# Attention and two MLPs on one core: the first two heads prepared one at a time, their similarities computed in token rows, the order of the first slots rewritten

## The chip, the cores and the metric

The kernel runs on one core of one Trainium2 chip. The metric is the device time of one execution in microseconds (us).

## The reference

The inputs are q, k, v of shape (2, 8, 768, 64), 16 centroids for each of the 8 heads, and the weights of two MLPs; part of the inputs is scaled by 8.

```python
q_assign = argmax(einsum(q / |q|, centroids / |centroids|))    # per token, of 16 clusters; k_assign alike
mask = q_assign[..., :, None] == k_assign[..., None, :]
scores = where(mask, 0.125 * q @ k.T, -1e9)
attn = softmax(scores) @ v                                     # 16 heads of 768 tokens
x = attn as (1536, 512)
x = ((x @ w1) * (x @ w2)) @ w3 @ w_out                         # d_ff 1024
out = softplus(x @ w_in) @ w_o2                                # d_ff 2048
```

## The kernel before

The program has three stages: attention over 16 heads, in 8 pairs; the first MLP; the second. While attention runs, w3 @ w_out is multiplied out once (24 pieces of weights, `wseq`), so that the first MLP has one product less. The MLP stages are not touched by the change.

**One head** has two tiles, `q` and `k` (`QT`, `KT`), of 128 partitions by 2 by 768. In plane 0, rows 0 to 63 hold the high parts of the transposed q or k, rows 64 to 95 a part of the low parts, and rows 96 to 127 the mask rows (one-hot cluster numbers, scaled by 2**100 on one side, so that pairs of tokens of different clusters get a huge score). Plane 1 holds the rest of the low parts, and row 96 of `q` there takes the row minima.

**Preparing a pair.** `load_qk` loads raw q and k (tile `rawqk`); `t1_pe` transposes them on TensorE in four units (head j, half of the tokens), and `t1_ev` splits each into `H` (ScalarE) and `L` (VectorE, L321). `t_dma` copies `H` and `L` into the rows of `q` and `k` by seven DMAs a head (1.15 MB) on SP's queue. `norm_sq`, `norm_sum`, `norm_root` and `norm_rec` make the inverse norms. `sims_pe` multiplies `H` and `L` of both heads with the centroids (`cst`), `sims_ev` copies the result to `sT`, `simsT_pe` turns it into token rows, `assign` finds the first cluster with the largest value (L406 to L420, VectorE) and writes the one-hot tile `oh`, `back_pe` transposes it, `back_ev` scales it into `sg`, and `m_dma` copies `sg` into the mask rows of both heads. Head 0 alone gets plane 0 by engine copies (`t_first`), and its mask rows are written by ScalarE straight from PSUM (L438).

**The slots.** Attention is written out by hand as a loop over 106 slots s. A head has six slots, each for 128 queries: `mx_pe(s)` (L623, their scores against all keys, into `mb`, or `sb` for odd s below 9) and `mx_red(s)` (L632, VectorE: their row minimum). Nine slots later (ML = 9) come `st_pe` (L653, transposed scores of that slot's share, into `sb`) and `st_exp` (L660, ScalarE), and one more slot later `av_pe` (L668, times v). After a head's six minima, `m_row` transposes them and a DMA puts them into row 96 of `q`; `st_pe` of that head needs it. The tables `PE1`, `EV1` say in which slot pair 1 is prepared, `PE`, `EV` (by `steps`) the same for the later pairs. `w_step` advances the 24 weight pieces from slot 9 on, a new piece every 2.5 slots; `w_load` loads them (0.5 MB each). From slot 76 (`WSLOT`) on, the first weights of the MLP are decoded.

Everything inside this loop keeps the written order on each engine; SP's queue issues its DMAs in the written order too. Three PSUM banks (`rb`) are handed around by `take` and `give`, first given, first taken.

Of the kernel before, what the change touches and what calls it, by code (L numbers as in the profile page):

```python
# [27 lines left out]
def fused_kernel(ctx: ExitStack, tc, q, k, v, centroids, w1, w2, w3, wo, w_in, w_o2, out):  # L28
# [175 lines left out]
    def centroid_load():  # L204
        PR["cw"] = ap1.tile([P, D], F32, name="cw")
        dma_in(PR["cw"], centroids.rearrange("h c d -> (h c) d"))

    def centroid_prep():
# [24 lines left out]

    def centroid_turn():
# [4 lines left out]
        for ni, sc in enumerate((-8.0, 1.0)):  # L239
            rows = slice(64 * ni, 64 * ni + 64)  # L240
            mv = m[rows, :P].rearrange("p (g j c) -> p g j c", j=2, c=NCL)
            cv = cst[rows].rearrange("p (g j) x -> p g j x", j=2)
            for j in range(2):
                o = 64 * ni + 32 * j
                hi, lo = cv[:, :, j, o : o + NCL], cv[:, :, j, o + NCL : o + 2 * NCL]
                nc.vector.tensor_scalar(
                    out=hi, in0=mv[:, :, j, :], scalar1=sc, scalar2=None, op0=ALU.mult
                )
                nc.vector.scalar_tensor_tensor(
                    out=lo, in0=mv[:, :, j, :], scalar=sc, in1=f32(hi),  # L250
                    op0=ALU.mult, op1=ALU.subtract,
                )
# [27 lines left out]
    def norm_root(pi):  # L280

        fl = PR["n", pi].rearrange("p t c n j -> p t (c n j)")
        nc.vector.tensor_scalar_max(fl[:, 1], fl[:, 0], 1e-30)
        nc.scalar.activation(fl[:, 2], fl[:, 1], AF.Ln)
        nc.scalar.activation(fl[:, 1], fl[:, 2], AF.Exp, scale=0.5)

    def norm_rec(pi, i):
        fl = PR["n", pi].rearrange("p t c n j -> p t (c n j)")
        if i == 0:
            nc.vector.reciprocal(fl[:, 2], fl[:, 1])  # L290
        elif i == 1:
            nc.gpsimd.tensor_tensor(out=fl[:, 0], in0=fl[:, 0], in1=fl[:, 2], op=ALU.mult)
            nc.gpsimd.tensor_tensor(out=fl[:, 0], in0=fl[:, 0], in1=fl[:, 1], op=ALU.add)
        else:
            nc.vector.tensor_scalar(
                out=fl[:, 2], in0=fl[:, 0], scalar1=0.5, scalar2=1e-6,
                op0=ALU.mult, op1=ALU.add,
            )
            nc.vector.reciprocal(fl[:, 3], fl[:, 2])

    def t1_pe(pi, u):
# [5 lines left out]
        m = take()  # L307
# [7 lines left out]
    def t1_ev(pi, u):  # L315
# [881 lines left out]
```

## Time and profile before

| | us |
|---|---|
| three runs | 842.25, 843.08, 843.41 |
| median | 843.08 |
| profiled execution | 842.76 |
| its span | 840.9 |
| TensorE busy in the span | 796.8 (95%) |
| VectorE, ScalarE, GpSimd busy | 450.6, 396.5, 240.7 |

The span lies inside the execution's time: 1.86 us of the 842.76 are outside it. TensorE (PE) is busy for 95% of the span; the page's line of forty slices (21 us each) shows where it is not: the digits start with 3, 6, 7, 9, stand at 9 after that, and end with 7.

### The profile page before, as it was taken

Reading aid. Unit: us, or ns where it says so; the run is one execution under the profiler, and the core shown is the slowest. Engines: PE = TensorE matmul, PEld = TensorE weight load, DVE = VectorE, ACT = ScalarE, POOL = GpSimd, SP = SyncE. Lnnn points to the kernel's source line nnn. Section 1 sums busy time; section 2 is a strip of 40 time slices with the busy share of each in tenths; the row PEclk is TensorE's granted clock in tenths of the full one; section 3 lists DMA queues with packets and bytes.
Section 4 is the critical chain, followed back from the end, with each engine's and each line's share of the span. In section 5 each row is a group of like instructions: output and inputs, shape, how many; then the busy total and the mean of one; then the engine's idle time right before and its main releaser. Section 6 shows DMA issues by size and latency. Waiting matters only on the chain.

```text
span 840.9 us, 10003 instructions
## 1 busy us (share of the span) xinstructions
PE 796.8 (95%) x3553; PEld 635.5 (76%) x3553; DVE 450.6 (54%) x754; ACT 396.5 (47%) x683; POOL 240.7 (29%) x232
## 2 busy tenths in 40 slices
PE   3679999989999999999999999999998999999997
PEld 2457777867777777778888888887786888888886
DVE  5867565475756565335332343345878644454443
ACT  3345445455453445455333245345555544454443
POOL 4145241245223122145201213222444222222220
PEclk9679999999999999999999999999999999999999
DMA  6875665465552564026301224330210100001001
GB/s 162 203 154 154 161 147 161 122 148 157 152 121 67 133 156 120 21 90 204 127 1 50 83 69 130 120 101 1 75 51 1 50 1 1 1 12 39 1 0 51
DMA packets 77490, 75.60 MB, mean 90 GB/s; under 512 B 46336, under 2 KB 62848, under 8 KB 77440
## 3 DMA queue, kind: packets, MB, share of 16 engines
q1 hardware_dynamic: 75476, 73.84, 32.5%
q10 hardware_dynamic: 1964, 1.12, 0.5%
q8 instruction: 28, 0.46, 0.2%
q14 instruction: 22, 0.18, 0.1%
HBM read 50.41 MB, written 3.24 MB: 64 GB/s over the span
## 4 chain that ended last, share of the span: by engine, by line
PE 77%; DVE 13%; DMA 3%; ACT 3%; SPq 2%; issue 2%; POOL 1%; DVEq 0%; ACTq 0%; POOLq 0%
PE avb L668 11%; PE rb L834 8%; PE sb L834 8%; PE sb L653 6%; PE sb L1059 6%; PE mb L1128 6%; PE rb L1059 5%; PE rb L533 5%; PE mb L856 4%; PE mb L623 3%; PE rb L1128 3%; PE avb L1128 3%; DVE mn L632 2%; PE avb L856 2%; PE rb L856 2%
## 5 line engine op out<-in xcount | busy, mean ns | idle before, releaser
L668 PE MATMUL avb<-E,v 128*128 128x384 f32 x384 | 142.7, 494 | 0.4 <-ACT t L61 0.4
L632 DVE TENSOR_REDUCE mn<-mb 128x1 f32<-128x768 f32 x92 | 87.7, 953 | 103.4 <-PE mb L623 103.0
L76 POOL TENSOR_TENSOR u<-u,t 128x512 f32<-128x512 f32 x47 | 66.2, 1409 | 173.1 <-DVE u L1082 173.1
L660 ACT ACTIVATE E<-sb 128x768 f32<-128x768 f32 x96 | 77.6, 808 | 70.1 <-PE sb L653 69.2
L653 PE MATMUL sb<-q,k 128*128 128x384 f32 (+1 forms) x384 | 91.4, 361 | 4.5 <-ACT E L660 4.5
L668 PEld LDWEIGHTS avb<-E,v 128*128 128x128 f32 x384 | 71.9, 192 | 28.7 <-ACT t L61 2.3
L653 PEld LDWEIGHTS sb<-q,k 128*128 128x128 f32 (+1 forms) x384 | 67.3, 194 | 9.6 <-ACT E L660 7.2
L623 PE MATMUL mb<-k,q 128*128 128x384 f32 x184 | 65.9, 440 | 8.0 <-DVE mn L632 4.1
L1059 PE MATMUL sb<-ys,wh_i 128*128 128x512 f32 x192 | 64.1, 395 | 3.6 <-ACT t L1070 2.9
L1072 DVE TENSOR_SCALAR u<-t 128x512 f32<-128x512 f32 x48 | 25.5, 531 | 71.3 <-ACT t L1071 71.3
L1059 PE MATMUL rb<-ys,wh_i 128*128 128x512 f32 x192 | 63.4, 392 | 0.0
L834 PE MATMUL rb<-xs,wh 128*128 128x512 f32 x192 | 61.7, 393 | 0.0
L834 PE MATMUL sb<-xs,wh 128*128 128x512 f32 x192 | 61.7, 392 | 0.0
L76 POOL TENSOR_TENSOR wl_o<-d_o,wh_o 128x512 fp32r<-128x512 f32 x16 | 21.2, 1327 | 122.3 <-ACT wh_o L61 116.2
L623 PEld LDWEIGHTS mb<-k,q 128*128 128x128 f32 x184 | 34.1, 198 | 26.7 <-DVE mn L632 7.2
L1081 ACT ACTIVATE u<-u 128x512 f32<-128x512 f32 x48 | 30.4, 633 | 42.4 <-DVE t L1078 42.2
L715 POOL TENSOR_TENSOR xT<-t,R 64x384 f32<-64x384 f32 x32 | 33.3, 1061 | 52.6 <-DMA R<-rd 52.3
L79 DVE TENSOR_TENSOR gl<-u,gh 128x512 fp32r<-128x512 f32 x48 | 37.8, 788 | 15.7 <-ACT gh L61 15.2
L1059 PEld LDWEIGHTS sb<-ys,wh_i 128*128 128x128 f32 x192 | 35.9, 188 | 13.3 <-ACT t L1070 3.9
L1059 PEld LDWEIGHTS rb<-ys,wh_i 128*128 128x128 f32 x192 | 36.1, 188 | 8.0
L834 PEld LDWEIGHTS rb<-xs,wh 128*128 128x128 f32 x192 | 36.1, 188 | 7.8
L834 PEld LDWEIGHTS sb<-xs,wh 128*128 128x128 f32 x192 | 36.1, 188 | 7.8
(202 smaller groups left out, 1730.9 us busy)
## 6 DMA issues: line engine op xcount, KB each, us to landing
w3r<-in_moe_w_dram SPq DMA_DIRECT2D x16, 512.0 KB
w12r<-in_moe_w_dram SPq DMA_DIRECT2D x16, 512.0 KB
wir<-in_moe_w_in_dram SPq DMA_DIRECT2D x16, 512.0 KB
wor<-in_moe_w_out_dram SPq DMA_DIRECT2D x16, 512.0 KB
q<-H SPq DMA_DIRECT2D x15, 384.0 KB
w3r<-in_moe_w_out_dram SPq DMA_DIRECT2D x8, 512.0 KB
k<-L SPq DMA_DIRECT2D x16, 192.0 KB
v<-in_v_dram SPq DMA_DIRECT2D x16, 192.0 KB
```

The costliest lines, as they stand in the source:

```text
L76: nc.gpsimd.tensor_tensor(out=o, in0=i, in1=hi, op=ALU.subtract)
L79: return nc.vector.tensor_tensor(out=o, in0=i, in1=hi, op=ALU.subtract)
L533: nc.tensor.matmul(m, a[:, ks], bb, start=(mc == 0 and x == 0), stop=(mc == NK - 1 and x == 2))
L623: nc.tensor.matmul(bank[:, hf, :HALF], QT[g][:, 0, c * P : (c + 1) * P], KT[g][:, 0, hf * HALF : (hf + 1) * HALF], start=True, stop=True,)
L632: nc.vector.tensor_reduce(out=MN[g][:, c : c + 1], in_=mx_bank(s)[:, :, :HALF], op=ALU.min, axis=AX.XY)
L653: nc.tensor.matmul(sbank[:, i, :HALF], KT[g][: P - 31 * n, n, ks], QT[g][: P - 31 * n, n, qs], start=(n == 0), stop=(n == 1),)
L660: nc.scalar.activation(E[j], sbank[:, :, :HALF], AF.Exp, scale=-1.0)
L668: nc.tensor.matmul(avbank[:, :HALF], V[g][:, 2 * kp + i, :], e[:, i, :], start=(kp == 0 and i == 0), stop=(kp == 2 and i == 1),)
L834: nc.tensor.matmul(bk[:, :BLK], a[:, sl], bb, start=(n == 0), stop=(n == 3 * CC - 1))
L856: nc.tensor.matmul(ybank[e][:, :BLK], a[:, es], bb, start=(fc == 0 and n == 0), stop=(fc == NFC - 1 and n == 2),)
L1059: nc.tensor.matmul(hbank[(bl * NF2 + fc) % 4][:, :BLK], a[:, sl], bb, start=(n == 0), stop=(n == 3 * CC - 1))
L1128: nc.tensor.matmul(ob, a[:, sl], bb, start=(fc == 0 and n == 0), stop=(fc == NF2 - 1 and n == 2),)
```

## The change

- The first pair is prepared head by head. Head 0's similarities come from 18 small products (`sims_first`: 128 tokens against 32 columns of centroids, written straight in token rows), with no `sT` copy and no `simsT_pe`; then its inverse norms and `assign` on 192 columns instead of 384. Head 1 follows in the steps 0 to 6 of the loop.
- `back_first` writes the mask rows of heads 0 and 1 straight from PSUM, the first half of the tokens by ScalarE, the second by VectorE. Plane 0 of head 0 is now filled by DMAs (`t_dma(0, 0, [0])`); `t_first` is gone.
- The loop runs over 104 steps o. Steps 0 to 5 do the minima of head 0, step 6 the row of minima; step 7 starts `st_pe`; the minima of slots 6 to 11 are done two to a step in steps 8 to 10, those of 12 to 19 two to a step in steps 15 to 18; steps 11 to 14 have none. From step 19 on it is one a step, slot s = o + 1. The lag `ML` is 8.
- Pair 1 is prepared in steps 8 to 14 (before: slots 0 to 10), pair 2 in steps 13 to 21. The weight pieces start at step 16, one every 2.25 steps, and the MLP's weights are decoded from step 83.
- `spin(n)` adds n products of the identity with itself into `mb`, whose result nobody reads: 26 ahead of the first transposes, 16 before `assign`, 6 in each of steps 1 to 5.
- The centroids are loaded on ScalarE's queue; three weight pieces and v are queued on SP before head 1's copies; a tile of its own holds the first quarter of the second batch's x.

```diff
-        dma_in(PR["cw"], centroids.rearrange("h c d -> (h c) d"))
+        nc.scalar.dma_start(PR["cw"], centroids.rearrange("h c d -> (h c) d"))
...
+    def t_dma(pi, j, ns=range(2)):
 
 
 
         hd = 2 * pi + j
         a, l = f32(PR["H", j]), f32(PR["L", j])
-        if hd:
+        if ns[0] == 0:
             t_tiles(hd)
         qt, kt = QT[hd], KT[hd]
         dma = nc.sync.dma_start
-        if hd:
-            dma(f32(qt[:D]), a[:D].unsqueeze(1).to_broadcast([D, 2, S]))
-            dma(f32(kt[:D, 0, :]), a[D:])
-        else:
-            dma(f32(qt[:D, 1, :]), a[:D])
-        dma(f32(kt[:D, 1, :]), l[D:])
-        for n in range(2 if hd else 1):
-            n = 1 - n
+        for n in ns:
+            if n == 0:
+                dma(f32(qt[:D]), a[:D].unsqueeze(1).to_broadcast([D, 2, S]))
+            dma(f32(kt[:D, n, :]), l[D:] if n else a[D:])
...
+    def sims_first(j, cs):
+
+        if cs[0] == 0:
+            PR["sx"] = take()
+        w = cst[:, j].rearrange("p (n j t b) -> p n j t b", n=2, j=2, t=2)
+        for c in cs:
+            for i, (x, t) in enumerate((("H", 0), ("H", 1), ("L", 0))):
+                nc.tensor.matmul(
+                    PR["sx"][:, c * 2 * NCL : (c + 1) * 2 * NCL],
+                    PR[x, j][:, c * P : (c + 1) * P], w[:, :, j, t],
+                    start=(i == 0), stop=(i == 2),
+                )
+
...
+    def back_first(j):
+
+        for hf in range(2):
+            m = take()
+            mb = m.bitcast(BF16)
+            for c in range(3):
+                nc.tensor.transpose(mb[:, c * P : (c + 1) * P], oh[:, 3 * hf + c, :], identB)
+            sl = slice(hf * HALF, (hf + 1) * HALF)
+            for ni, d in enumerate((QT, KT)):
+                r = slice(64 * ni + 32 * j, 64 * ni + 32 * j + 32)
+                if hf:
+                    nc.vector.tensor_scalar(
+                        out=d[j][96:, 0, sl], in0=mb[r, :HALF], scalar1=bigcol[r, 0:1],
+                        scalar2=None, op0=ALU.mult,
+                    )
+                else:
+                    nc.scalar.activation(
+                        d[j][96:, 0, sl], mb[r, :HALF], AF.Copy, scale=bigcol[r, 0:1]
+                    )
+            give(m)
+
+    def spin(n):
+
+        for _ in range(n):
+            nc.tensor.matmul(mbank[:, 1, :P], identB, identB, start=True, stop=True)
+
...
-            for x in WT[wseq[n][0]].get(k - 5 * n // 2, ""):
+            for x in WT[wseq[n][0]].get(k - 9 * n // 4, ""):
...
-    ML = 9
+    ML = 8
...
+    PE0 = {
+        1: [(sims_first, 1, range(3))], 2: [(sims_first, 1, range(3, 6))],
+    }
+    EV0 = {
+        0: [(norm_root, 0, 1)], 1: [(norm_rec, 0, 0, 1), (norm_rec, 0, 1, 1)],
+        2: [(norm_rec, 0, 2, 1)], 6: [(assign, 0, 0, 1), (assign, 0, 1, 1), (back_first, 1)],
+    }
     PE1 = {
-        0: [(t1_pe, 0)], 1: [(t1_pe, 1)], 2: [(t1_pe, 2)], 3: [(t1_pe, 3)], 4: [(sims_pe, 0)],
-        5: [(sims_pe, 1)], 6: [(simsT_pe,)], 9: [(back_pe,)],
+        8: [(t1_pe, 1, 0)], 9: [(t1_pe, 1, 1)], 10: [(t1_pe, 1, 2)], 11: [(t1_pe, 1, 3)],
+        12: [(sims_pe, 1, 0), (sims_pe, 1, 1)], 13: [(simsT_pe, 1)], 14: [(back_pe, 1)],
     }
     EV1 = {
-        0: [(t1_ev, 0), (norm_sq, 0)], 1: [(t1_ev, 1), (norm_sum, 0)], 2: [(t1_ev, 2), (norm_sq, 1), (t_dma, 0)],
-        3: [(t1_ev, 3), (norm_sum, 1), (norm_root,)], 4: [(sims_ev, 0), (norm_rec, 0), (norm_rec, 1)],
-        5: [(sims_ev, 1), (norm_rec, 2), (t_dma, 1)], 7: [(assign, 0)], 8: [(assign, 1)],
-        9: [(back_ev,)], 10: [(m_dma, 0), (m_dma, 1)],
+        8: [(t1_ev, 1, 0), (norm_sq, 1, 0)], 9: [(t1_ev, 1, 1), (norm_sq, 1, 1)],
+        10: [(t1_ev, 1, 2), (norm_sum, 1, 0), (t_dma, 1, 0)],
+        11: [(t1_ev, 1, 3), (norm_sum, 1, 1), (norm_root, 1)],
+        12: [(sims_ev, 1, 0), (sims_ev, 1, 1), (norm_rec, 1, 0), (norm_rec, 1, 1), (t_dma, 1, 1)],
+        13: [(norm_rec, 1, 2), (assign, 1, 0), (assign, 1, 1)],
+        14: [(back_ev, 1), (m_dma, 1, 0), (m_dma, 1, 1)],
     }
+    PE2 = {
+        14: [(t1_pe, 2, 0)], 15: [(t1_pe, 2, 1)], 16: [(t1_pe, 2, 2)], 17: [(t1_pe, 2, 3)],
+        18: [(sims_pe, 2, 0), (sims_pe, 2, 1)], 19: [(simsT_pe, 2)], 21: [(back_pe, 2)],
+    }
+    EV2 = {
+        13: [(norm_sq, 2, 0), (norm_fold, 2, 0)], 14: [(t1_ev, 2, 0), (norm_sq, 2, 1), (norm_fold, 2, 1)],
+        15: [(t1_ev, 2, 1), (norm_sum, 2, 0)], 16: [(t1_ev, 2, 2), (norm_sum, 2, 1), (norm_root, 2), (t_dma, 2, 0)],
+        17: [(t1_ev, 2, 3), (norm_rec, 2, 0), (norm_rec, 2, 1)],
+        18: [(sims_ev, 2, 0), (sims_ev, 2, 1), (norm_rec, 2, 2), (t_dma, 2, 1)],
+        19: [(assign, 2, 0)], 20: [(assign, 2, 1)], 21: [(back_ev, 2), (m_dma, 2, 0), (m_dma, 2, 1)],
+        24: [(load_v, 2)],
+    }
...
-    WSLOT = 76
-    W0 = 4
-    wk = [W0]
+    WSLOT = 83
+    W1 = 16
+    wk = [0]
...
-        w_load()
-        w_load()
-        t1_pe(0, 0)
-        t1_pe(0, 1)
+        spin(26)
         centroid_prep()
-        t1_ev(0, 0)
-        t1_ev(0, 1)
-        t1_pe(0, 2)
-        t1_pe(0, 3)
-        t1_ev(0, 2)
-        t1_ev(0, 3)
-        centroid_turn()
         norm_sq(0, 0)
         norm_sq(0, 1)
+        t1_pe(0, 0)
+        t1_ev(0, 0)
+        centroid_turn()
+        t1_pe(0, 1)
+        t1_pe(0, 2, avbank)
+        t1_pe(0, 3, sbank[:, 1, :])
+        t1_hi(0, 1)
+        norm_sum(0, 0)
+        t1_lo(0, 1)
+        t1_hi(0, 2)
+        t1_hi(0, 3)
+        sims_first(0, range(QC))
+        norm_root(0, 0)
+        t_dma(0, 0, [0])
         load_qk(1)
-        t_first()
-        sims_pe(0, 0)
-        sims_pe(0, 1)
-        sims_ev(0, 0)
-        sims_ev(0, 1)
-        norm_sum(0, 0)
+        t_dma(0, 0, [1])
+        norm_rec(0, 0, 0)
+        norm_rec(0, 1, 0)
+        norm_rec(0, 2, 0)
+        for _ in range(3):
+            w_load()
+        load_v(0)
+        spin(16)
+        assign(0, 0, 0)
+        assign(0, 1, 0)
+        t1_lo(0, 2)
+        back_first(0)
+        t1_lo(0, 3)
+        t_dma(0, 1)
         norm_sum(0, 1)
-        simsT_pe(0)
-        norm_root(0)
-        for n in range(W0):
-            w_step(n, WALL[:1])
-        norm_rec(0, 0)
-        norm_rec(0, 1)
-        norm_rec(0, 2)
-        t_dma(0, 1)
-        t_dma(0, 0)
-        assign(0, 0)
-        assign(0, 1)
-        back_pe(0)
-        back_ev(0)
-        m_dma(0, 1, act_dma)
-        w_load()
-        load_v(0)
-        for n in range(W0):
-            w_step(n, WALL[1:])
-        for s in range(NSLOT + ML + AL):
-            j = s - ML
+        firsts = [[i] for i in range(6)] + [[], [], [6, 7], [8, 9], [10, 11]] + [[]] * 4
+        firsts += [[12, 13], [14, 15], [16, 17], [18, 19]]
+        rows = {6: 0, 11: 1, 18: 2}
+        for o in range(NSLOT + ML + AL - 1):
+            s = o + 1 if o >= len(firsts) else -100
+            mxs = firsts[o] if s < 0 else [s] if s < NSLOT else []
+            j = o - ML + 1
             a = j - AL
-            if s < NSLOT:
-                mx_pe(s)
-                mx_red(s)
-            if s and s % QC == 0 and s <= NSLOT:
-                m_row(s // QC - 1)
-            weights = s >= ML
+            if a > 0 and a % 3 == 0:
+                av_ev(a // 3 - 1)
+            if o in rows:
+                m_row(rows[o])
+            for i in mxs[:1]:
+                mx_pe(i)
+                mx_red(i)
+            weights = o >= W1
             if weights:
                 w_step(wk[0], "hlpqe")
-            if a > 0 and a % 3 == 0:
-                av_ev(a // 3 - 1)
-            for tab in (PE1, EV1):
-                for f, *x in tab.get(s, ()):
-                    f(1, *x)
-            if s == 4:
+            if s > 0 and s % QC == 0 and s <= NSLOT:
+                m_row(s // QC - 1)
+            for tab in (PE0, EV0, PE1, EV1, PE2, EV2):
+                for f, *x in tab.get(o, ()):
+                    f(*x)
+            if 1 <= o < 6:
+                spin(6)
+            if o == 7:
+                load_v(1)
+            if o == 12:
                 load_qk(2)
-            if s == 8:
-                load_v(1)
+            if o == 17:
+                load_qk(3)
             steps(PE, s)
             steps(EV, s)
             if 0 <= j < NSLOT:
                 st_pe(j)
                 st_exp(j)
+            for i in mxs[1:]:
+                mx_pe(i)
+                mx_red(i)
             if weights:
                 w_step(wk[0], "Abds")
             if 0 <= a:
@@ -974,7 +1048,7 @@
```

Two places where the order of instructions changes:

**SP's queue (DMAs), between the loads of pair 1 and the copies of head 1** (`q0`, `k0` are head 0's tiles, `q1`, `k1` head 1's; `H0_1` is the high part of pair 0's head 1). Before:

```order
L346 DMA k1_250<-H0_1_182 32x768
L341 DMA q0_212<-H0_0_158 64x768
L342 DMA k0_213<-L0_0_159 64x768
L345 DMA q0_212<-L0_0_159 32x768
L346 DMA k0_213<-H0_0_158 32x768
L91 DMA w3r2_283<-in_moe_w_out_dram 128x1024
L588 DMA v0_0_285<-in_v_dram 128x6x64
```

With the change:

```order
L362 DMA k0_248<-H0_0_197 32x768
L91 DMA w3r0_267<-in_moe_w_out_dram 128x1024
L91 DMA w3r1_269<-in_moe_w_out_dram 128x1024
L91 DMA w3r2_271<-in_moe_w_out_dram 128x1024
L633 DMA v0_0_273<-in_v_dram 128x6x64
L633 DMA v0_1_276<-in_v_dram 128x6x64
L359 DMA q1_315<-H0_1_212 64x2x768
L360 DMA k1_316<-H0_1_212 64x768
```

Head 1's copies stood ahead of head 0's and of all but two weight loads; they now stand behind head 0's, three weight loads and v.

**PE at the first minima of head 2** (`k2`, `q2`; the tiles whose mask rows come through `sg`). Before, slot 11's end and slot 12:

```order
L309 MATMUL rb0_100<-identF_58,rawqk2_366 128x128 x3
L653 MATMUL sb_97<-q0_212,k0_213 128x384 x4
L668 MATMUL avb_99<-E1_486,v0_0_285 128x384 x2
L623 MATMUL mb_98<-k2_333,q2_332 128x384 x2
L639 MATMUL rb1_101<-identF_58,mn1_393 6x128
```

With the change, step 14 and the start of step 15:

```order
L455 MATMUL rb1_101<-identB_63,oh_143 128x128
L319 MATMUL rb0_100<-identF_58,rawqk2_562 128x128 x3
L698 MATMUL sb_97<-q1_315,k1_316 128x384 x4
L713 MATMUL avb_99<-E6_599,v0_1_276 128x384 x2
L668 MATMUL mb_98<-k2_493,q2_492 128x384 x2
L319 MATMUL rb2_102<-identF_58,rawqk2_562 128x128 x3
```

Before, two `av_pe` (E0, E1) and three `st_pe` stood ahead of head 2's first product; now seven `av_pe` (E0 to E6) and eight `st_pe` do, and three of pair 2's four transposes have moved behind it.

## Rows read from the trace of the kernel before

**Rows 1.** Busy time by stretch: us, each engine busy (instructions), TensorE's granted clock, DMA share, GB/s.
```profile
0.00:10.00 10.00, 2.39 (x9) 1.64 (x9) 3.31 (x30) 3.31 (x6) 4.98 (x11) 1.00 0.72 187
10.00:20.00 10.00, 5.45 (x24) 4.43 (x24) 6.92 (x18) 4.55 (x9) 3.49 (x6) 1.00 0.63 132
20.00:30.00 10.00, 2.95 (x14) 2.55 (x15) 6.86 (x13) 2.80 (x4) 2.30 (x5) 0.57 0.78 199
30.00:40.00 10.00, 7.92 (x35) 6.02 (x33) 9.24 (x14) 5.21 (x11) 1.20 (x3) 0.74 0.86 208
40.00:50.00 10.00, 6.38 (x34) 5.20 (x34) 8.96 (x17) 2.54 (x4) 6.27 (x8) 0.77 1.04 198
50.00:60.00 10.00, 8.07 (x33) 6.28 (x32) 5.56 (x11) 4.94 (x11) 2.24 (x3) 0.84 0.60 133
60.00:80.00 20.00, 19.64 (x86) 14.51 (x85) 11.94 (x20) 10.64 (x18) 8.63 (x9) 0.94 0.56 144
```

**Rows 2.** Chain that ended last, 0 to 60 us: start, us, what.
```profile
1.48 4.62 DMA rawqk<-in_k_dram
...
39.65 1.29 PE rb L393 x12
...
51.49 6.41 DMA k<-sg
...
58.03 0.58 PE mb L623 x2
```

**Rows 3.** Timeline of VectorE: start, us, line, operation, tiles.
```profile
9.72 1.83 DVE L230 TENSOR_SCALAR cn<-cw,cs 128x64 f32<-128x64 f32 x2
...
21.32 0.57 DVE L406 TENSOR_TENSOR rb<-rb,nrm 128x384 f32<-128x384 f32 x1
...
24.31 0.62 DVE L420 TENSOR_TENSOR oh<-rb,mx 128x192 bf16<-128x192 f32 x2
...
28.86 0.96 DVE L632 TENSOR_REDUCE mn<-mb 128x1 f32<-128x768 f32 x1 [2.46 <-PE mb L623]
```

**Rows 4.** Timeline of ScalarE and its DMA queue (ACTq).
```profile
25.91 0.89 ACT L438 ACTIVATE q<-rb,bigcol 32x768 fp32r<-32x768 bf16 x1 [5.79 <-PE rb L430]
...
28.66 0.63 ACTq L448 DMA_DIRECT2D q<-sg  x1
...
39.98 1.34 ACTq L643 DMA_DIRECT2D q<-mr  x1
```

**Rows 5.** Timeline of SP's DMA queue.
```profile
25.75 5.71 SPq L588 DMA_DIRECT2D v<-in_v_dram  x2
...
43.85 0.52 SPq L339 DMA_DIRECT2D k<-H  x1
```

**Rows 6.** Waits of SP's queue, 0 to 100 us: total, times, longest.
```profile
SPq L588 <- DMA q<-sg: 4.5, 1, 4.5
...
SPq L339 <- DMA q<-mr: 1.5, 1, 1.5
```

**Rows 7.** Timeline of PE: the third `st_pe` and the second `av_pe`.
```profile
53.86 0.95 PE L653 MATMUL sb<-q,k 128*128 128x384 f32 x4
54.65 1.46 PE L668 MATMUL avb<-E,v 128*128 128x384 f32 x4
```

**Rows 8.** Chain that ended last, 335 to 400 us: one slot at full clock.
```profile
347.67 0.35 PE mb L623 x2
348.02 0.70 PE sb L653 x4
348.72 1.29 PE avb L668 x4
```

**Rows 9.** Chain that ended last, 170 to 200 us: prices of preparing a pair.
```profile
175.52 0.35 PE rb L430 x6
...
178.28 0.33 PE rb L309 x3
...
197.97 0.93 PE rb L373 x4
```

More of the change, by code (lines that the diff above doesn't have):

```diff
@@ L237, in centroid_turn @@
         nc.tensor.transpose(m[:, :P], cn.rearrange("p t d -> p (t d)"), identF)
-        for ni, sc in enumerate((-8.0, 1.0)):
+        parts = []
+        for ni in range(2):
             rows = slice(64 * ni, 64 * ni + 64)
             mv = m[rows, :P].rearrange("p (g j c) -> p g j c", j=2, c=NCL)
[L242 to L252, printed above, removed]
+            c = cst[rows]
+            part = [c.ap[0], (2 * P, H // 2), (P + 32, 2), (1, NCL)]
+            hi, lo = (bass.AP(c.tensor, c.offset + 64 * ni + t * NCL, part) for t in range(2))
+            hi, lo = hi.bitcast(F32R), lo.bitcast(F32R)
+            act_copy(hi, mv)
+            parts.append((hi, lo, mv))
+        for hi, lo, mv in parts:
+            dve_sub(lo, mv, f32(hi))
         give(m)
@@ L278, in norm_sum, with norm_root, norm_rows, norm_rec @@
         )
[L280 to L288, printed above, removed]
+    def norm_root(pi, j=None):
+        fl = norm_rows(pi, j)
+        nc.vector.tensor_scalar_max(fl[1], fl[0], 1e-30)
+        nc.scalar.activation(fl[2], fl[1], AF.Ln)
+        nc.scalar.activation(fl[1], fl[2], AF.Exp, scale=0.5)
+    def norm_rows(pi, j):
+        n = PR["n", pi]
+        if j is None:
+            return [n[:, t].rearrange("p c n j -> p (c n j)") for t in range(4)]
+        return [n[:, t, :, :, j].rearrange("p c n -> p (c n)") for t in range(4)]
+    def norm_rec(pi, i, j=None):
+        fl = norm_rows(pi, j)
         if i == 0:
[L290 removed]
+            nc.vector.reciprocal(fl[2], fl[1])
         elif i == 1:
[L292 to L293 removed]
+            e = nc.gpsimd if j is None else nc.vector
+            e.tensor_tensor(out=fl[0], in0=fl[0], in1=fl[2], op=ALU.mult)
+            e.tensor_tensor(out=fl[0], in0=fl[0], in1=fl[1], op=ALU.add)
         else:
             nc.vector.tensor_scalar(
[L296 to L301 removed]
+                out=fl[2], in0=fl[0], scalar1=0.5, scalar2=1e-6, op0=ALU.mult, op1=ALU.add
+            )
+            nc.vector.reciprocal(fl[3], fl[2])
+    def t1_pe(pi, u, bank=None):
         j, hf = divmod(u, 2)
@@ L306, in t1_pe @@
                 PR[x, j] = ap1.tile([P, S], F32R, tag=f"{x}{j}", name=f"{x}{pi}_{j}")
-        m = take()
+        m = take() if bank is None else bank
         for i in range(3):
@@ L709, in x_norm @@
         b, h = divmod(g, H)
-        if b not in XT:
-            assert wk[0] > NWSTEP - 4
-            XT[b] = xp_.tile([P, CC, S], F32, tag="x1", name="xT1")
+        if b and h == 2 and hf == 0:
+            assert wk[0] >= NWSTEP
+            XT[1] = xp_.tile([P, CC - 1, S], F32, tag="x1", name="xT1")
         rs = slice(D * (h % 2), D * (h % 2) + D)
@@ L872, in steps @@
     def steps(tab, s):
-        for pi in range(2, NPAIR):
+        for pi in range(3, NPAIR):
             for d in (0, 2):
                 for f, *a in tab.get(s - 2 * QC * pi - d, ()):
-                    if (d == 2) == (pi == 2 and f in NORM) and (f is not load_qk or pi > 2):
+                    if (d == 2) == (pi == 3 and f in NORM) and (f is not load_qk or pi > 3):
                         f(pi, *a)
+    PE0 = {
+        1: [(sims_first, 1, range(3))], 2: [(sims_first, 1, range(3, 6))],
+    }
```

95 lines of the change are left out of this document (50 added, 45 removed).

## The prediction

> **What bounds the kernel now.** I read the busy times by stretch first, then the chain that ended last, then the timelines of the engines around its long pieces. After 60 us PE is busy nearly all the time, so work there costs its full PE time; the first 60 us are different. PE is busy 2.39 + 5.45 + 2.95 + 7.92 + 6.38 + 8.07 = 33.2 us of those 60 [rows 1]: 26.8 us are idle, and much of the rest ran at a granted clock between 0.57 and 0.84, that is partly at the 1.2 GHz level. The chain shows who holds PE up: the first loads (4.62 us), VectorE's work on the first pair, and last the copy of pair 1's mask rows, k<-sg, which took 6.41 us from issue to landing and let head 2's first product start only at 58.03 [rows 2]. By then PE had done three `st_pe` and two `av_pe`: the third `st_pe` starts at 53.86, the second `av_pe` at 54.65 [rows 7]. The DMA queues are the other bound there: from 20 to 50 us they move 199, 208 and 198 GB/s at shares of 0.78 to 1.04 [rows 1].
>
> So I compare both programs at one event, head 2's first product, and ask two things: when does it come, and how much PE work already lies behind it. Behind it the work is the same, at the same prices: 0.35 us for a slot's minima products, 0.70 for `st_pe`, 1.29 for `av_pe` [rows 8]; 0.33 for a unit of transposes, 0.35 for `back_pe`, 0.93 + 0.47 (half as wide) for `sims_pe` [rows 9]; 1.29 for `simsT_pe` [rows 2].
>
> **The change, part by part.**
>
> *First minimum.* Before, VectorE has the centroids' norm at 9.72 + 1.83 = 11.55, runs `assign` from 21.32 to 24.93 and starts the first minimum at 28.86 [rows 3], after ScalarE has written two mask rows of 0.89 us each [rows 4]. Now the centroids stand first in ScalarE's queue, the first half of the loads alone is needed, one norm sum and two of four splits stand ahead of `assign`, and `assign` has half the columns: 3.6 us become about 1.9. The mask rows are halved between two engines: 1.8 us become 0.9. I estimate the centroids 3 us earlier, the end of `assign` at 15, and the first minimum at 18.7 because a split and the second head's norm sum stand ahead of it. It can't come before the copies of plane 0 have landed (0.77 MB from 10 us on at 200 GB/s is 3.8 us, and 2 to 4 us to land, so 16), and if only the pieces just named were saved (3 + 1.7 + 0.9 us) it would come at 23.3.
>
> *The new small products.* No product of 32 columns is in the trace. The nearest row is `simsT_pe`, six products of 64 columns in 1.29 us, 0.215 each [rows 2]. The bounds for 18 products are a quarter of that price and, at half clock, double: 1.0 to 7.7 us; I take 0.13 each, 2.3 us. Half of them wait for the second half's split, and they lie beside the norm chain on VectorE and ScalarE, so I cost them at nothing up to 2 us; if that cover is gone, the first minimum moves by the rest.
>
> *The idle products.* An identity product of 128 columns costs 0.35 / 6 = 0.06 us at full clock [rows 9], 0.12 at half: 26 of them take 3.1 us and end at about 6, as the first loads land; 16 more lie in the wait for `assign`. The six in each step are not free. They write into `mb`, the bank of the even slots' minima products, so in steps 2 and 4 they wait until VectorE has read it, and the next slot's product stands behind them: 6 x 0.06 to 0.12 plus 0.35 to 0.7 us, about 0.8 each, 1.6 in all, less in the gaps that VectorE fills with head 1's norms.
>
> *Minima of head 0 and the start of `st_pe`.* Six minima at 0.96 [rows 3] are 5.8 us, head 1's norm steps 1.0, the two waits 1.6: from 18.7 to 27.1. Then the transpose and its copy (0.6), and the DMA into row 96. Before, that DMA was issued at 39.98 [rows 4], and a copy that had waited for it in SP's queue went out at 43.85 [rows 5, 6]: 3.9 us. So `st_pe` starts at 31.6. Head 1's `assign` lies in that wait.
>
> *Head 1's copies.* The product of slot 6 stands right behind the first `st_pe`, and needs `q1` and `k1`. Their first four DMAs stand behind 0.77 MB for head 0's plane 0, 0.77 of raw pair 1, 0.38 for plane 1, three weight pieces (1.54) and v (0.38): with their own 0.77 MB that is 4.6 MB from 10 us on. At 200 GB/s [rows 1] they are there at 33. This ends later than the minima by 0.7 us, so slot 6 is at 33.0.
>
> *Steps 8 to 14.* PE: three steps of 2 x 0.35 + 0.70 + 1.29 + 0.33 = 3.02 (9.1), step 11 with 2.4, step 12 with 1.40 + 1.99 = 3.4: 47.9. `simsT_pe` 1.3, then `assign` of 384 columns 3.6 (only 1.99 us of PE work covers it), `back_pe` 0.35: 53.1. ScalarE's `sg` 0.9, the first mask copy's issue 0.63: the second one starts at 54.6. What is late next is its landing. Bounds: q<-sg of pair 0, issued at 28.66 [rows 4], held the second v load in SP's queue for 4.5 of that group's 5.71 us, until about 30.9 [rows 5, 6]: 2.2 us; k<-sg took 6.4 [rows 2]. So head 2's first product comes between 56.8 and 61.0; I take the middle, 59.0, since pair 2's raw loads are still in the queue.
>
> *What lies behind it.* In the changed order eight `st_pe` and seven `av_pe` are done by then instead of three and two: 5 x (0.70 + 1.29) = 9.95 us, less three units of pair 2's transposes that are still to come (1.0): 9.0 us less is left.
>
> The Trainium skill, page DMA: Bandwidth & Descriptors, section Anatomy of one DMA, puts the fixed cost of a DMA at about 2.0 us, and by it the product would come at 56.6 and the time would be 832.6. The traced 2.2 agrees with that on a nearly idle queue, 3.9 and 6.4 do not, so the trace's middle is used.
>
> *Weights.* A piece every 2.25 steps instead of 2.5, from step 16, is the same PE work in fewer steps. The banks are taken sooner after they are given: twice, in the second half of the pieces, a row of minima or `simsT_pe` takes a bank that VectorE is to clear in the same step, behind a minimum of 0.96: about 1.3 us each, 2.6. Against that, 60 to 80 us before had 0.36 us of idle PE and a clock of 0.94 [rows 1], that is 12% of 20 us at half clock, 1.2 us lost, which PE may keep now. I let these cancel and keep 3 us either way.
>
> **The sum.** The event comes 59.0 - 58.0 = 1.0 us later and 9.0 us less stand behind it: 8.0 us gained. On the profiled execution, 842.76 (its span 840.9 and 1.86 around it), that is 834.7; the median of the runs, 843.08, is 0.3 higher, so 835.0.
>
> **The rivals.**
>
> *A, the copies are prompt.* If loads and copies land as fast as the best traced one, slot 6 is at 31.6 and head 2's first product at 55.4: 9.0 + 2.6 = 11.6, and with 2 us of kept clock 829.5 to 831.5. For it speaks that weight pieces, rows of 4 KB, are long ones among small packets; against it the share of 0.78 to 1.04 [rows 1].
>
> *B, given back.* The steps from 16 to 32 carry no weight products yet, but three pairs' copies and loads; PE waits for them as it did at 58.03, and the denser pieces add bank waits: 8 us of waits in all leave 843.
>
> *C, slower: the queue starves head 1.* Head 1's copies come behind 1.54 MB of weights that nobody needs before step 18, and PE, which keeps its order, stands at slot 6 with `st_pe` behind it. Each us after 33.0 is a us lost; from 41 on the change loses. That needs under 150 GB/s. The lowest stretch of the busy part is 133 [rows 1]: then the copies land at 10 + 34.6 = 44.6 and the time is 835.0 + 11.6 = 846.6. Against it stand the three stretches near 200. The same page's section Queues, rings and completion order says that descriptors of a ring are taken in order, which is this rival's mechanism; the trace shows an order on SP's queue, and not how far small copies pass large ones.
>
> *D, the products behind the idle ones* wait longer than I sum: it delays the minima, but the copies at 33.0 cover the first 1.4 us of it. It lies within the forecast.
>
> **How the numbers follow.** The forecast (832 to 838.5: the landing's bounds and the 3 us of weights) has 0.58, A 0.27, B 0.07, C 0.08. The range from 828.5 to 841 takes in A and the forecast's upper edge, and leaves out most of B and C. A measurement can tell about 0.2%, 1.7 us. Faster by more than that: 0.58 + 0.27 and a little of B, 0.86; within it 0.06, most of B; slower 0.08, C.
>
> **What would show it.** Right: the first minimum near 19 where it was at 28.9 [rows 3], the first `st_pe` near 32; head 2's first product near 59 with eight `st_pe` ahead of it; PE's idle time in the first 60 us near 20 where it was 26.8. In steps 2 and 4 the idle products wait for VectorE's minimum. Wrong: slot 6 waiting past 36 for a copy of head 1 (C); PE idle or at half clock between 60 and 110 us by more than 5 us (B); head 2's first product before 57 (A). If the first minimum comes after 24, the prologue is not what I summed.

## The result, and the profile after

| | median, us | ratio to before, 95% interval |
|---|---|---|
| before (4 runs beside it) | 842.66 | |
| changed | 853.95 (850.7 to 854.91) | 1.0131 (1.0098 to 1.0164) |

The change makes the kernel 1.3% slower; 835.0 was forecast. The profiled execution of the changed kernel took 850.7 us with a span of 848.9, so 8.0 us more span than before are to be found in its trace. It is the fastest of the four runs; the other 3.3 us of the 11.3 between the two medians are in no trace.

The busy times by stretch answer to [rows 1] up to 80 us and then go on. Columns as there.

```profile
0.00:10.00 10.00, 6.20 (x50) 5.57 (x50) 5.14 (x36) 4.16 (x9) 6.47 (x13) 1.00 0.43 85
10.00:20.00 10.00, 5.58 (x39) 4.68 (x39) 8.55 (x22) 1.63 (x5) 3.04 (x6) 0.66 0.99 220
20.00:30.00 10.00, 8.25 (x53) 7.20 (x52) 5.57 (x11) 0.37 (x2) 0.00 (x0) 0.65 1.05 263
30.00:40.00 10.00, 7.96 (x35) 6.71 (x34) 6.51 (x13) 4.76 (x8) 0.00 (x0) 0.66 0.28 68
40.00:50.00 10.00, 9.46 (x43) 6.43 (x41) 6.99 (x11) 5.39 (x12) 0.17 (x1) 1.00 0.61 143
50.00:60.00 10.00, 8.26 (x45) 6.16 (x45) 5.15 (x10) 4.95 (x9) 3.64 (x6) 1.00 0.73 174
...
200.00:250.00 50.00, 43.04 (x208) 32.74 (x207) 31.58 (x53) 23.88 (x42) 23.07 (x25) 1.00 0.74 179
250.00:300.00 50.00, 47.16 (x231) 37.17 (x230) 29.93 (x54) 22.42 (x39) 9.25 (x13) 1.00 0.24 61
300.00:350.00 50.00, 44.95 (x188) 33.09 (x186) 25.77 (x39) 21.40 (x33) 7.96 (x9) 0.97 0.48 123
```

The same late stretches of the kernel before:

```profile
200.00:250.00 50.00, 49.41 (x244) 39.10 (x243) 33.16 (x60) 25.05 (x44) 13.53 (x17) 1.00 0.57 142
250.00:300.00 50.00, 48.80 (x239) 38.60 (x238) 27.03 (x47) 20.49 (x36) 13.15 (x17) 1.00 0.42 104
300.00:350.00 50.00, 49.01 (x215) 36.76 (x214) 30.89 (x47) 26.66 (x41) 12.24 (x13) 1.00 0.41 102
```

Read the first number behind each stretch's length, PE's busy time. The first 60 us improved: 45.7 us busy, where before it was 33.2 [rows 1]; but 7.5 us of the 45.7 are the 72 idle products, which compute nothing. The loss is later. From 200 to 250 us PE does 43.0 us of work where it did 49.4, and from 300 to 350 us 45.0 where it did 49.0. Added up over all stretches from 60 to 350 us, PE stands idle for 20.9 us against 8.9 before, 12.1 more. All of it lies behind 200 us: from 60 to 200 us PE is busy for 133.9 us in both programs.

Two events fix the bookkeeping. Head 2's first product:

```profile
61.78 0.59 PE L668 MATMUL mb<-k,q 128*128 128x384 f32 x2 [1.59 <-DMA k<-sg]
```

It comes 3.75 us later than before (58.03, [rows 2]) with the 9.0 us less work behind it that the prediction counted: 5.3 us ahead. (In x1 below, the same program up to here, it came at 63.08, 4.0 us ahead.) And the first product of the first MLP, here in the changed kernel (a group's row: count, durations in ns, first and last start) and behind it before:

```profile
L879 PE MATMUL rb<-xs,wh x77: 387/389/686, 375.5 to 449.7; 128*128 128x512 f32 x77
```

```profile
368.22 0.69 PE L834 MATMUL rb<-xs,wh 128*128 128x512 f32 x1
```

It is 7.3 us late. So the change was 5.3 us ahead at 62 us and lost 12.6 us between there and 375 us; the 12.1 us of added idle time are nearly all of it. After that the two programs take the same time to within 0.7 us.

**Where PE stands late.** At 333 us it waits 4.5 us for VectorE's minima. The timeline of VectorE shows that VectorE itself stood:

```profile
330.97 1.19 DVE L738 TENSOR_SCALAR r<-r 128x6 f32<-128x6 f32 x1 [5.68 <-DMA r<-sd]
```

`r` is a head's row sums on their way back from memory; a small DMA, for which the minima behind it on VectorE wait too. SP's queue says why it is late:

```profile
312.82 1.51 SPq L91 DMA_DIRECT2D w12r<-in_moe_w_dram  x3
...
325.94 0.38 SPq L726 DMA_DIRECT2D sd<-t  x1
329.30 0.37 SPq L733 DMA_DIRECT2D r<-sd  x1
```

The first three loads of the MLP's weights (1.5 MB) are issued in one step, as soon as the last weight piece is done. The later start and the other spacing of the pieces move that step right in front of pair 7's copies (the first is issued at 314.44), and everything behind them is late: `sd<-t` is issued at 325.94, and `r<-sd`, which needs it, only at 329.30. Before, the same three loads had their step 11 us ahead of those copies:

```profile
290.33 1.52 SPq L91 DMA_DIRECT2D w12r<-in_moe_w_dram  x3
...
301.91 0.66 SPq L338 DMA_DIRECT2D q<-H  x1
```

The stand between 200 and 226 us reads the same way in the chain that ended last:

```profile
206.97 4.35 DMA r<-sd
...
216.45 6.03 DMA k<-H
...
222.50 2.61 DMA R<-rd
...
225.11 0.56 ACT H L327
225.68 0.71 ACT E L705
```

Three transfers in turn: `r`, which VectorE waits for; one of a head's copies out of `H`; and `R<-rd` (192 KB), issued behind those copies. As it lands, ScalarE writes the next `H` (L327), and the exponential (L705) that PE needs stands behind that write. The profile names `R<-rd` as what released the write; by the program it is the copies out of the old `H` that must be over first, and their last was issued at 220.43 on the same queue. Which of the two landed last the trace doesn't tell. The waits of PE in 200 to 300 us show the other kind, a bank that VectorE must clear first:

```profile
PE rb L684 <- DVE w3ol L79: 1.6, 1, 1.6
PE rb L410 <- DVE w3ol L79: 1.6, 1, 1.6
```

Together they are 3.2 us of the 9.8 that PE stood idle from 200 to 300 us; before, it stood 1.8 us there in all.

One thing to know when its times are read: the changed kernel leaves out the squares of head 6 and their fold (pair 3's first head), because no step has the slot number that calls for them. GpSimd's timeline shows a single square of pair 3 (78.52) ahead of pair 4's first (108.48); before, two stood there, at 68.15 and 77.80:

```profile
78.52 1.47 POOL L262 TENSOR_TENSOR sq<-rawqk 128x768 f32<-128x768 f32 x1 [2.67 <-PE rb L410]
108.48 1.47 POOL L262 TENSOR_TENSOR sq<-rawqk 128x768 f32<-128x768 f32 x1
```

### The profile page after: what moved, and what is told of

It reads as the page before. It is cut to its first block, busy times and chain, and to the rows that moved or that the text cites. A ratio compares the mean times of both kernels' runs of the same rounds, so it can differ in the third digit from the quotient of the medians.

```text
span 848.9 us, 10198 instructions
## 1 busy us (share of the span) xinstructions
PE 805.6 (95%) x3647; PEld 641.7 (76%) x3647; DVE 452.1 (53%) x767; ACT 395.2 (47%) x684; POOL 236.2 (28%) x225
## 4 chain that ended last, share of the span: by engine, by line
PE 79%; DVE 11%; DMA 4%; ACT 3%; issue 2%; SPq 1%; POOL 1%; ACTq 0%; DVEq 0%; POOLq 0%
PE avb L713 11%; PE rb L879 8%; PE sb L879 8%; PE sb L1134 6%; PE sb L698 6%; PE rb L1134 6%; PE mb L1203 6%; PE rb L578 5%; PE mb L901 4%; PE mb L668 4%; PE rb L1203 3%; PE avb L1203 3%; PE avb L901 2%; PE rb L901 2%; DVE mn L677 2%
## 5 line engine op out<-in xcount | busy, mean ns | idle before, releaser
L705 ACT ACTIVATE E<-sb 128x768 f32<-128x768 f32 x96 | 77.6, 809 | 70.2 <-PE sb L698 69.2
L668 PE MATMUL mb<-k,q 128*128 128x384 f32 x186 | 66.1, 437 | 12.6 <-DVE mn L677 8.2
L760 POOL TENSOR_TENSOR xT<-t,R 64x384 f32<-64x384 f32 x32 | 35.7, 1135 | 99.4 <-DMA R<-rd 87.8
L668 PEld LDWEIGHTS mb<-k,q 128*128 128x128 f32 x186 | 33.6, 197 | 35.7 <-DVE mn L677 17.1
```

Of the source, the lines that this page charges most:

```text
L668: nc.tensor.matmul(bank[:, hf, :HALF], QT[g][:, 0, c * P : (c + 1) * P], KT[g][:, 0, hf * HALF : (hf + 1) * HALF], start=True, stop=True,)
L705: nc.scalar.activation(E[j], sbank[:, :, :HALF], AF.Exp, scale=-1.0)
```

## The experiments

Three theories stood against each other. T: the early gain is real and is lost late, to the step of the three loads and to the pieces' spacing, both in the queue's order. S: the idle products cost it. (In the expectations the two parts of T are called the burst and the density theory, and S stands under the prologue theory.) C: the copies of head 1 starve slot 6, as the prediction's rival had it; the trace alone ends that one, since slot 6 starts at 34.20 right behind the first `st_pe` (32.77), and waits for nothing.

| run | what | median, us | ratio to before |
|---|---|---|---|
| x1 | three loads later, one at a time | 846.05 | 1.005 (1.0035 to 1.0065) |
| x5 | spacing and first step of the pieces alone | 845.25 | 1.003 (1.001 to 1.005) |
| x2 | x1 and the spacing | 839.75 | 0.9973 (0.9958 to 0.9989) |
| b1 | before, its three loads in a later step | 846.84 | 1.0054 (1.0035 to 1.0073) |
| x3 | changed, no idle products | 849.41 | 1.0094 (1.0063 to 1.0125) |
| x4 | changed, none in the steps | 852.31 | 1.0114 (1.0087 to 1.0141) |
| y1 | x2, no idle products | 838.95 | 0.9961 (0.9938 to 0.9983) |
| y2 | y1, head 2's minima on ACT's queue | 835.75 | 0.9914 (0.989 to 0.9939) |
| y3 | y2, pair 2's mask rows too | 834.52 | 0.990 (0.9873 to 0.9928) |
| z1 | y3, head 6's squares done | 836.15 | 0.9916 (0.9888 to 0.9944) |
| z2 | z1, the first 26 idle products | 834.64 | 0.990 (0.9876 to 0.9924) |

Before took 842.56, 842.29 and 843.12 us beside the three groups (x1, x2, x3, b1; x4, y1 to y3; x5, z1, z2).

**x1: the three loads apart and later.**

```diff
-            if wk[0] == NWSTEP:
-                feed.load(3)
+            if o in (80, 82, 84):
+                feed.load(1)
-    WSLOT = 83
+    WSLOT = 87
```

> The changed kernel, but the three MLP weight loads go out one at a time in steps 80, 82 and 84 instead of together behind step 77, and their decoding starts at step 87 instead of 83. Burst theory: in the changed kernel VectorE stood 5.7 us for r<-sd at 331, because 1.5 MB of loads and 1.5 MB of pair 7's copies were queued ahead of it; the 4.5 us that PE waited there, and the half clock behind it (1.5 us), go: 848 to 850 us (changed: 854). Density theory (the pieces at 2.25 steps cost it all): no change, 853 to 855. Prologue theory (idle products and half clock in the first 60 us): no change either.

7.9 us less than the changed kernel, and 2 us below the band of its theory. Of its late stretches the last is repaired, the first is not:

```profile
200.00:250.00 50.00, 42.89 (x209) 32.84 (x209) 32.89 (x53) 23.11 (x40) 22.91 (x25) 1.00 0.72 177
...
300.00:350.00 50.00, 49.14 (x219) 37.15 (x218) 27.50 (x41) 23.52 (x37) 6.70 (x8) 1.00 0.46 118
```

The load step thus accounts for 4.2 us of PE's time here (45.0 to 49.1) and 0.3 us behind 350 us, about what lies between the two profiled executions (850.7 and 846.21). The rest of the 7.9 is in no trace, since the changed kernel was profiled in its fastest run. The edit also moves the decoding by four steps, which was not tried apart.

**b1: the same step in the kernel before.** The opposite edit: the kernel before, with its three loads put right ahead of a pair's copies.

```diff
-            if wk[0] == NWSTEP:
+            if s == 79:
                 feed.load(3)
-    WSLOT = 76
+    WSLOT = 85
```

> The kernel before, with its three MLP weight loads moved from behind slot 72 to behind slot 79, where pair 7's copies are queued next, and their decoding from slot 76 to 85. Burst theory: the stand of the changed kernel appears here too, VectorE waiting for r<-sd or ScalarE for a copy: 4 to 6 us slower than before, 847 to 849. Prologue and density theory: no change, 842 to 844.

4.3 us slower, with nothing of the change in it, though the decoding moved as well. The wait is the changed kernel's, but smaller, and the kernel before had some of it already. Waits of VectorE and of PE, 300 to 350 us, before:

```profile
DVE r L693 <- DMA r<-sd: 3.5, 2, 3.0
...
PE mb L623 <- DVE mn L632: 1.0, 1, 1.0
```

and in b1:

```profile
DVE r L693 <- DMA r<-sd: 4.3, 2, 3.8
...
PE mb L623 <- DVE mn L632: 2.5, 1, 2.5
```

PE does 47.31 us of work there instead of 49.01, 1.7 of the 2.2 us between the two profiled executions. So the place of the three loads costs time in both kernels: 1.7 us of PE's time here, 4.2 in the changed one.

**x2 and x5: the spacing of the pieces,** with the loads moved (x2) and alone (x5).

```diff
-            for x in WT[wseq[n][0]].get(k - 9 * n // 4, ""):
+            for x in WT[wseq[n][0]].get(k - 5 * n // 2, ""):
-    NWSTEP = 9 * (NW - 1) // 4 + 11
+    NWSTEP = 5 * (NW - 1) // 2 + 11
-    W1 = 16
+    W1 = 13
```

> As the run before, and the weight pieces come every 2.5 steps from step 13 instead of every 2.25 from step 16. Density theory: the waits of PE for VectorE's w3ol (1.65 twice) go, and with the loads 10% further apart the stand at 205 to 226 us (5.5 us of idle PE) shrinks: 842 to 845 us. Burst theory: bank waits go, but the stand at 205 to 226 only moves: 846 to 848. Prologue theory: no change against the run before; or worse, as weights start while pair 1's copies are queued.

> This is the changed kernel with one of the two repairs alone: the weights' pieces two and a half steps apart and from step 13 on, and the last three loads still in one step (now step 79). With both repairs the kernel took 839.75 us, with the loads alone 846.05, with none 853.95. Theory: the two losses lie in different stretches (200 to 300 us, and 300 to 350 us) and add, so this takes 846 to 849, with TensorE near 48.9 us busy between 200 and 250 us, and a stand of 3 to 5 us behind the three loads. Rival: both losses are one lateness, and whichever repair comes first takes all of it: 840 to 842.

In x2 the stands of 200 to 300 us are gone:

```profile
200.00:250.00 50.00, 48.85 (x242) 38.20 (x241) 31.07 (x52) 27.00 (x47) 25.72 (x27) 1.00 0.73 175
```

and the bank waits `w3ol` no longer stand among PE's waits. Its time is 2.3 us below the band of its theory. x5 repairs the same stretch and keeps the other:

```profile
200.00:250.00 50.00, 48.87 (x241) 38.20 (x240) 31.93 (x53) 26.73 (x47) 26.43 (x28) 1.00 0.73 173
...
300.00:350.00 50.00, 46.14 (x196) 34.82 (x195) 25.45 (x39) 22.73 (x36) 7.99 (x9) 0.97 0.39 105
```

In x5 the pieces end later, so the three loads now stand behind pair 7's copies (the last out of `H` is issued at 316.58, the last mask row at 317.86) and not ahead of them. VectorE's stand for `r` is there all the same, because `r<-sd`, issued at 321.62, now has the loads directly ahead of it:

```profile
319.63 1.51 SPq L91 DMA_DIRECT2D w12r<-in_moe_w_dram  x3
...
328.15 0.17 DVE L738 TENSOR_SCALAR r<-r 128x6 f32<-128x6 f32 x1 [5.80 <-DMA r<-sd]
```

In x1 a single load stands there, and the wait is 1.3 us. So the three loads in one step, ahead of the small transfer, are what VectorE's stands for `r` in the changed kernel and in x5 have in common; a pair's copies between them are not needed.

Alone the loads are worth 7.9 us, the spacing 8.7, both together 14.2, so the two losses are distinct and nearly add; x5 came out 0.8 us below its band. The edit moves two numbers at once (the spacing and the first step), and which of them does it was not tried apart, nor how much of the repair is the bank waits and how much the transfers. With both repaired, the change beats the kernel before by 0.27%: T holds. Both open a new stand, at 60 to 100 us (31.2 us busy of 40 in x2, 30.8 in x5); in x2:

```profile
85.65 1.30 PE L698 MATMUL sb<-q,k 97*128 97x384 f32 x3 [5.46 <-DMA q<-mr]
```

**x3 and x4: the idle products,** all left out (x3), and only those of the steps (x4, the last edit alone).

```diff
-        spin(26)
...
-        spin(16)
...
-            if 1 <= o < 6:
-                spin(6)
```

> The changed kernel without any idle product (26, 16 and 5 times 6 taken out); nothing that is computed changes. Prologue theory: head 2's first product, at 61.8 us, comes 3 us earlier (five groups of 0.67 us stand in PE's chain between 20.9 and 28.4), and the whole is 3 us faster, 851. If the idle products keep the clock up, as they are meant to, the first 45 us run at half clock and the whole is 1 to 3 us slower. Burst and density theory: within 2 us of 854 either way, and the stands at 205 to 226 and at 333 are there unchanged.

> This is the changed kernel without the six idle products in each of steps 1 to 5; the 26 at the start and the 16 ahead of the first minima stay. Without any idle products the kernel took 849.4 us, with all of them 853.95. Theory: those in the steps stand between the products of minima while TensorE is the engine that sets the pace and runs at its lower level, at about 0.67 us a group (five groups, 3.3 us less the pauses that they fill), so most of the 4.5 us comes from them: 850 to 851.5. Rival: they stand in pauses that the minima leave anyway, and the 4.5 us come from the 16 ahead of the first minimum, which must go before it: then 853 to 854 here. Either way the granted clock between 20 and 40 us is below 0.75, since with none and with all it was about 0.65.

S explains at most a part of the loss. x3 is 4.5 us below the changed kernel by the medians, lower than any of its theories had it, and the intervals of the two overlap; it still has both late stands (44.35 us busy in 200 to 250, 44.73 in 300 to 350). Its head 2 starts at 58.87, the place that was forecast, but that is one execution: without any idle product too, it starts at 61.50, 63.35 and 62.82 in y1, y2 and y3, with all of them at 61.78 and 63.08 (changed, x1), and without those in the steps at 62.56 (x4). x4's theory and rival both fail to fit: 1.6 us, between them, and its median is inside the runs of the changed kernel. The first minimum is at 17.1 in x3, x4 and the changed kernel, so the 16 ahead of it delay nothing. What the remaining 2.9 us between x3 and x4 are is open; in the profiles the clock came back earlier in x3 (0.81 in 30 to 40 us, 0.54 in x4), one profile each. What is shown is that the idle products don't keep the clock up: with all of them TensorE's granted clock was 0.65 to 0.66 from 10 to 40 us, and 0.50 from 20 to 30 us in x1 and x2; half of full speed is the 1.2 GHz level.

**y1, y2, y3: the new stand at 60 to 100 us.** y1 is x2 without idle products. y2 and y3 change the queue of a few small copies:

```diff
-        (nc.sync if g else nc.scalar).dma_start(f32(QT[g][96:97, 1, :]), f32(t))
+        (nc.scalar if g in (0, 2) else nc.sync).dma_start(f32(QT[g][96:97, 1, :]), f32(t))
...
-        ... (m_dma, 2, 0), (m_dma, 2, 1)],
+        ... (m_dma, 2, 0, nc.scalar.dma_start), (m_dma, 2, 1, nc.scalar.dma_start)],
```

> This joins two runs: the weights' pieces two and a half steps apart again and the last three loads at steps 80, 82 and 84 (839.75 us), and no idle products (849.4 against 853.95 for the kernel with them, so 4.5 us less). Theory: what the idle products cost lies before the first steps of the attention and what the loads cost lies after 200 us, so the two add: 835 to 837. Rival: between 60 and 100 us TensorE waits for two transfers (the row of minima of head 2, 6.2 us, and the mask rows of pair 2, 5.7 us) that follow the queue's own dates, so an earlier start is waited off there: then 838 to 840, with TensorE's first product of head 2 near 60 and the stretch 60 to 100 still near 31 us busy.

> As the run before it, and the row of minima of head 2 goes out on ACT's queue instead of SP's, where it was issued right behind 2 MB of loads and landed 6.24 us later, with TensorE waiting 5.46 us for it at 85.7. Theory: its wait is the order of one queue, so on a queue of its own it lands in about 2 to 3 us and the wait falls to 1 to 2 us: 2 to 4 us less than the run before it. Rival: the loads fill all the DMA engines whatever the queue, so it lands 5 to 6 us after its issue there too: no change within 1 us.

> As the run before it, and the four mask rows of pair 2 go out on ACT's queue too; on SP's they were issued 1 us behind a load of 0.5 MB and the last landed 5.67 us later, with all of it on the chain of waits. Theory: 2 to 3 us less than the run before it, the last row landing 2 to 3 us after its issue. Rival: ACT, which does the exponentials, gives the time back at about 0.4 to 0.6 us for each issue (four issues, 2 us, ahead of an exponential that TensorE waits for): no change within 1 us.

y1 is the rival's case: 0.8 us of the 4.5 remain. Head 2 starts at 61.50, and the stands stay (chain of y1):

```profile
77.85 5.61 DMA q<-mr
...
93.19 5.19 DMA k<-sg
```

y2 brings 3.2 us, as its theory had it, and PE no longer waits for `q<-mr`. y3 brings another 1.2, between its theory (2 to 3) and its rival (within 1) and less than the measurement tells; but the copies did change. Issued on ACT's queue, the one that ends last is over in 2.58 us (chain of y3):

```profile
87.38 2.58 DMA k<-sg
```

**z1, z2: with head 6's squares done again.**

```diff
-        19: [(assign, 2, 0)],
+        19: [(assign, 2, 0), (norm_sq, 3, 0), (norm_fold, 3, 0)],
```

> As the kernel with rows and mask of pair 2 on ACT's queue (834.52 us), and the squares and the fold of head 6 (pair 3's first), which the changed kernel leaves out, are done again, in step 19. Two squares' worth of GpSimd, 1.5 us and about 1.6 us, before the second head's square in the same step. Theory: GpSimd is 10 to 15 us busy in 20 there and nothing waits for it within a slot: 834 to 835.5. Rival: the later sums hold the reciprocal roots and the assignment of pair 3, on DVE and TensorE: 836 to 838, with a wait of TensorE for the one-hot rows of pair 3.

> As the run before it, with the first 26 idle products kept (the 16 and those in the steps stay out). Without any idle product the profiles show the first small products of the similarities once at 0.37 us a pair (the upper level) and three times at 0.59 (the lower); with the 26 ahead of them always at 0.37. Theory: the 26 lie in a pause, so they cost nothing, and the small products take 2 us less when the clock is up: 0 to 2 us less than the run before it. Rival: the clock gives it back before the first minima at 17 us, which wait for the mask rows on ACT and not for TensorE: within 0.5 us of the run before it.

z1 is 1.6 us above y3, in its rival's band, and z2 1.5 below z1, in its theory's; the intervals overlap, so neither step is settled. z2 does all the work of the kernel before and is the version to keep: 1.0% under it. Its late stretches have no stand, and its 60 to 100 us have 34.3 us of work in 40:

```profile
60.00:100.00 40.00, 34.26 (x168) 25.47 (x167) 29.84 (x51) 20.54 (x38) 18.40 (x22) 1.00 0.69 168
...
300.00:350.00 50.00, 50.00 (x218) 37.84 (x217) 26.00 (x38) 27.24 (x42) 10.40 (x12) 1.00 0.40 109
```

## Why the prediction was wrong

Point by point, by its own steps:

- *First minimum*, 18.7 forecast: 17.10. The prologue's mechanism was right (the shorter `assign`, the halved mask rows, the earlier centroids).
- *Head 1's copies*, 33.0 forecast: they were there when they were needed. Slot 6 started at 34.20 behind `st_pe`, because DMA moved 220 and 263 GB/s between 10 and 30 us, not 200. Rival C did not occur.
- *The small products*, costed at nothing beside the norm chain: wrong for head 1's 18, which have no term in the sum of the minima. They stand between the minima, on PE, and the chain runs through them, at the lower clock 0.19 us each and not 0.13. *The idle products*, 1.6 us: in the chain they are four pieces, 2.5 us. Chain of the changed kernel, 19 to 28 us:

```profile
19.17 1.73 PE rb L399 x9
20.90 0.67 PE mb L482 x6
...
24.05 0.67 PE mb L482 x6
25.46 0.67 PE mb L482 x6
27.92 0.49 PE mb L482 x6
```

  In this stretch PE and not VectorE sets the pace, which the sum of "six minima at 0.96" had not allowed for. The minima end with the transpose at 29.88 instead of 27.1, and the start of `st_pe` at 32.77 instead of 31.6. What it stands behind is not the row's DMA: it is head 1's `assign` (29.82 to 32.14) and its transposes, which the prediction had put inside that wait.
- *Head 2's first product*, 59.0 (bounds 56.8 and 61.0): 61.78, late by 2.8 us, which is what two errors of opposite sign leave. Chain of the changed kernel:

```profile
35.76 1.28 PE sb L698 x4
...
52.37 1.30 PE rb L410 x12
...
59.53 2.12 DMA k<-sg
```

  The second mask copy went out at 59.53 and not at 54.6, 4.9 us late. Of these, slot 6 brought 1.2. Steps 8 to 12 brought 3.3: from slot 6 to `simsT_pe` they took 18.2 us, where the sum had 14.9 at the prices of the full clock; the granted clock was 0.66 until 40 us, and a `st_pe` there took 1.28 us and not 0.70. The landing gave 2.2 back: it took 2.12 us, near the lower of its two bounds, and not the middle, 4.3. So 5.3 us were gained at this event and not 8.0: the right sign, by terms that were mis-sized both ways.
- **The step that failed** is *What lies behind it* with *Weights*: "Behind it the work is the same, at the same prices", as *What bounds the kernel now* puts it, and "I let these cancel and keep 3 us either way". The work is the same; the waits are not. That step looked at the bank waits alone, priced at 2.6 us (3.2 were measured from 200 to 300 us), and at no DMA that the new spacing moves. The change moved a step of three loads to 1.6 us ahead of a pair's copies and put the pieces' loads among the transfers of the heads; 12.6 us were lost behind head 2's first product. Of the 16.0 us by which the profiled execution missed its forecast (850.7 for 834.7) that is the greater part; 2.8 are the late event, 0.7 lie in the MLPs. x1 and b1 show the three loads, x5 and x2 the pieces' spacing and first step; which transfer or bank wait carries how much of the second is read from the trace and not shown.
- *Rival B, given back*, is what happened, with its two causes (copies and loads, bank waits). It was put at the steps 16 to 32, where the loss was 2.5 us (PE idle 3.9 us in 60 to 100 us, 1.4 before) and was made up again by 200 us; all that stayed came in the steps behind. Its price of 8 us was too small and its chance of 0.07 was drawn from the wrong stretch.

With the late losses repaired and the work complete (z2) the median is 834.64, near the 835.0 that was forecast without them; but z2 also has two sets of copies on another queue and fewer idle products, so that agreement is no proof of the sum.

## What to carry to other kernels

When a change moves a counter that releases DMAs (a spacing, a first step, "when the last piece is done"), print SP's queue around every step that it moves, to the end of the loop, and look at what small copy stands behind each large load. Gains in the first steps of a pipeline are lost again at the next transfer with a date of its own; compare both programs at a second event late in the stage before counting them. A few small copies on which an engine waits are worth a queue without loads.

## What the runs showed of the hardware

- Small copies behind loads on one queue took 5.2 to 6.2 us from issue to the end of the wait (q<-mr 6.24 in x2 and 5.61 in y1, k<-sg 5.67 and 5.19, and 6.41 in the kernel before [rows 2], with a load issued 1.1 us ahead of it). The same k<-sg took 2.58 in y3 on ACT's queue, at 182 GB/s in that stretch (80 to 100 us), and pair 1's took 2.12 on SP's queue in the changed kernel, issued 4.5 us behind the last load. So a load directly ahead of them goes with the long wait. In y2 and y3 the copies on ACT's queue also left before the loads (q<-mr at 74.55, the loads from 75.88 on; k<-sg at 87.38, the load at 89.52); whether a copy on a queue of its own passes loads that are already moving, no run shows.
- The clock column can mislead at the start. In y1 it reads 1.00 from 10 us on (in y2, y3 and z1 too), while the products have the durations of the lower level:

```profile
10.00:20.00 10.00, 6.49 (x30) 5.66 (x30) 8.39 (x22) 1.57 (x4) 2.99 (x6) 1.00 0.91 213
```

```profile
10.17 0.59 PE L399 MATMUL rb<-cst,H 128*128 128x32 f32 x2
```

  The changed kernel has 0.38 for the same form at the same place, before the clock fell, and 0.59 after:

```profile
10.45 0.38 PE L399 MATMUL rb<-cst,H 128*128 128x32 f32 x2
...
19.46 0.59 PE L399 MATMUL rb<-cst,H 128*128 128x32 f32 x2
```

  There the duration of a known product is the better reading. By it, the four programs of the list without the 26 first idle products (y1, y2, y3, z1) run their first small products at the lower level throughout, and the changed kernel, with the 26, at the upper one; x3, without them, changes from 0.59 to 0.37 at 10 us.
